# Output stores moved from the SyncE to the GpSimd DMA queue in an FFT-mixing and gated-convolution kernel, with a new instruction order

## The chip, the cores and the metric

The kernel runs on one core of a Trainium2 chip. The core has a matrix engine (TensorE, PE in the profile; its weight loads are PEld), a vector engine (VectorE, DVE), a scalar engine (ScalarE, ACT), GpSimd (POOL) and a synchronisation engine (SyncE, SP), which computes nothing and here only issues DMA transfers. Sixteen DMA engines move the data between the chip's main memory (HBM) and the core's on-chip memory (SBUF); the matrix engine writes to accumulators (PSUM). The metric is the device time of one execution in microseconds (us), as the median of several runs.

## The reference

The input `x` has 8 batches of 3200 positions by 256 channels in float32. Two blocks follow each other. The first is a global filter: a real FFT along the positions, a multiplication with a complex filter, and the inverse FFT. The second is a gated linear unit with a causal convolution of 5 taps per channel:

```python
X = np.fft.rfft(x, axis=1)
y = np.fft.irfft(X * (filt_r + 1j * filt_i)[None], n=3200, axis=1)     # first block

yp = np.concatenate([zeros(B, 4, D), y], axis=1)                       # second block
gate_pre = sum(conv_w[k] * yp[:, k:k + S, :] for k in range(5))
gate = 1 / (1 + np.exp(-gate_pre))
out = (gate * (y @ w_val)) @ w_out                                     # float32
```

## The kernel before, in words

The FFT of 3200 points is done as 100 x 32 by matrix products with tables made on the chip. A batch runs through these stages; the short names are those of the planner and of the rank tables.

Input stages: `lx` loads x in 8 pieces of 100 partitions (`load_x`, L197; the DMA at L200 converts float32 to bfloat16) into one of 10 buffers `xt`. `s1` (PE, L467) is the product of length 100 with the tile's full 128 rows, `so` copies its result out of PSUM (ACT L458 or DVE L460), `t` transposes it on DVE (L486), `s2` (PE, L496, tiles of 64 x 64) is the product of length 32, `xs` copies it out. `z` (DVE, L512) multiplies with the filter.

Inverse stages: `ia` (PE, L527, 64 x 64) undoes the product of length 32, `ue` copies it out into `u`. The data then has to change its partitions. Batch 0 does that with a DVE transpose; batches 1 to 7 write `u` to a scratch tensor in HBM in 7 transfers (`wr`, `escr`, L550) and read it back in 8 pieces of two transfers each (`lv`, `vt`, L560 and L561). `ib` (PE, L578) is the inverse product of length 100, `ye` (ACT, L587) copies it to `yt`, whose halo of 4 columns GpSimd clears (`ha`, L594).

Output stages, in blocks of 512 positions, 7 per batch (the last has 128): `cv` (PE, L627, tiles of 32 x 32; the short block L613) is the convolution with diagonal tables, `ga` (ACT, L637) the sigmoid, `vl` (PE, L647) the product with `w_val`, `gv` (DVE, L662) the gate times it, `op` (PE, L670) the product with `w_out`, `oe` copies it out of PSUM into one of 4 buffers `o` (ACT or DVE), and `store` (L682; the DMA at L685) writes it to HBM, 512 KB for a full block.

The order is planned in Python when the kernel is built. `Plan` (L42) simulates the engines: each task has an engine or a choice of two (ACT or DVE for copies), an estimated duration, dependences, buffers that it takes and gives back, and a rank. Whenever an engine is free, the ready task of lowest rank goes next, and each engine's instructions are written out in that order; each engine then executes them strictly in order and waits where something isn't ready. The ranks are `8*batch + LAG[stage] + STEP[stage]*n`, with `FIRST` added for batch 0. `STAY` is added to a PE task whose tile shape (mode 0, 1 or 2 for full, 64 and 32) differs from the last one's, `LEAN` to a copy put on DVE. `CONV` is the planned duration of a convolution. DMA transfers are modelled too: issuing costs the issuing engine's time, and the transfer then occupies one resource `DQ` for its estimated duration. Its `mode` there tells the issuing queue, 0 for SP and 1 for POOL, and a transfer of the queue that did not go last is preferred. The helper `dma` (L697) adds such a transfer for SP; `dx` (L712) is that of an x load. Real transfers are not bound to this model.

Before the change POOL issues the x loads (and the filters and weights at the start), and SP issues scratch writes, scratch loads and output stores. An issuing engine that waits for a buffer or for a result holds back everything behind it in its order.

Of the kernel before, what the change touches and what calls it, by code (L numbers as in the profile page):

```python
# [20 lines left out]
NV = 4 * NS  # L21
TURN = (0,)

LAG = dict(lx=-196.5, s1=-215.5, so=-54.5, t=9.5, pd=-50, s2=-219, xs=-44.5, z=193.5, ia=60,
           ue=52.5, k=-194, ib=97, ye=-272, cv=79.5, ga=-241.5, vl=-22, gv=-253.5, op=152,
           oe=-151)
FIRST = dict(lx=-125.5, s1=102, so=31.5, t=257, pd=29, s2=41, xs=-256, z=-217, ia=-4.5, ue=25,
             k=20.5, ib=113, ye=135, cv=-14.5, ga=-103.5, vl=78, gv=-43.5, op=126, oe=145)
CONV = 1.14
STEP = dict(lx=0, s1=2.15, so=0.4, t=0.4, pd=0.3, s2=1.9, xs=0.4, z=0.8, ue=0.2, k=2.2, ib=2.45,  # L30
            ye=0.5, cv=2.4, ga=2, vl=1.15, gv=1.9, op=1.35, oe=0)
STAY, LEAN = 30.5, 87.5
RC = 4
NCH = R // RC
UCH = [(m, min(2, NM - m)) for m in range(0, NM, 2)]
# [104 lines left out]
def kernel(  # L140
# [21 lines left out]
    nc = tc.nc  # L162
# [6 lines left out]
    DQ = D // E  # L169
# [22 lines left out]
    st = {}  # L192
# [489 lines left out]
    def store(b, c):  # L682
        o = st.pop(("O", b, c))
        w = width(c)
        nc.sync.dma_start(  # L685
            out=out[b, BLK * c:BLK * c + w, :].rearrange("(p r) d -> p (r d)", p=128),
            in_=o[:, 0:w // 128 * D])

# [3 lines left out]
    add = plan.add  # L692
# [1 line left out]
    def two(a, v):  # L694
        return {"ACT": a, "DVE": v}

    def dma(name, us, rank, dep, give=(), land=2.0):  # L697
        add(name, {"DQ": us}, rank, dep, None, land=land, mode=0)
        add(name + "+", {"none": 0.0}, rank, [name], None, give=give)

    for b in range(B):
        turned = b in TURN
        t0 = NCH * b

        def at(stage, n=0, b=b, t0=t0):
            return t0 + LAG[stage] + (FIRST.get(stage, 0) if b == 0 else 0) + STEP.get(stage, 1) * n

        for j in range(NCH):
            if b:
                add(f"lx{b},{j}", {"POOL": 0.6}, at("lx", j), ["hold"],  # L710
                    lambda e, b=b, j=j: load_x(b, j), take=("xt",), land=1.5)
                add(f"dx{b},{j}", {"DQ": 1.15}, at("lx", j), [f"lx{b},{j}"], None, land=2.0, mode=1)  # L712
            dep = [f"dx{b},{j}"] if b else [f"x0{j}", "cfa"]
            dep = dep + ([f"s1{b},{j - 1}"] if j else [])
            add(f"s1{b},{j}", {"PE": 0.45}, at("s1", j), dep, lambda e, b=b, j=j: s1(b, j),
                ps=1, take=("so",) if j == 0 else (), give=("xt",), mode=0)
            add(f"so{b},{j}", two(0.93, 1.14), at("so", j), [f"s1{b},{j}"],
                lambda e, b=b, j=j: so(b, j, e), free=[(f"s1{b},{j}", 0)])
        for q in range(4):
            add(f"t{b},{q}", {"DVE": 1.17}, at("t"), [f"so{b},{j}" for j in range(NCH)]  # L720
                + ([f"t{b},{q - 1}"] if q else []),
                lambda e, b=b, q=q: turn(b, q), take=("t",) if q == 0 else (),
                give=("so",) if q == 3 else ())
        add(f"pd{b}", {"POOL": 1.2} if turned else {"none": 0.0}, at("pd"),
            ["pool"] + ([f"pd{b - 1}"] if b else []),
            lambda e, b=b: pad(b), take=("u",) if turned else ("u", "e"))
        for u, (m0, nm) in enumerate(UCH):
            half = 0 if m0 + nm <= FCUT[0][1] else 1
            add(f"s2{b},{u}", {"PE": 0.11 * nm}, at("s2", u), ["wa"]
                + [f"t{b},{q}" for q in range(4)] + ([f"s2{b},{u - 1}"] if u else []),  # L730
                lambda e, b=b, u=u: s2(b, u), ps=1, take=("xs", "z"),
                give=("t",) if u == len(UCH) - 1 else (), mode=1)
            add(f"xs{b},{u}", two(0.13 + 0.4 * nm, 0.04 + 0.55 * nm), at("xs", u),
                [f"s2{b},{u}"], lambda e, b=b, u=u: xs(b, u, e), free=[(f"s2{b},{u}", 0)])
            add(f"z{b},{u}", {"DVE": 0.06 + 0.55 * nm}, at("z", u), [f"xs{b},{u}", f"fl{half}"],
                lambda e, b=b, u=u: zed(b, u), give=("xs",))
            add(f"ia{b},{u}", {"PE": 0.22 * nm}, at("ia", u),
                [f"z{b},{u}", f"te{u // 2},1", f"pd{b}"],
                lambda e, b=b, u=u: inva(b, u), ps=1, give=("z",), mode=1)
            add(f"ue{b},{u}", two(0.13 + 0.4 * nm, 0.04 + 0.55 * nm), at("ue", u),  # L740
                [f"ia{b},{u}"], lambda e, b=b, u=u: ue(b, u, e), free=[(f"ia{b},{u}", 0)])
            if not turned:
                add(f"wr{b},{u}", {"SP": 0.45}, at("ue", u), [f"ue{b},{u}"],
                    lambda e, b=b, u=u: wr(b, u), land=1.0)
                dma(f"wq{b},{u}", 0.38 * nm, at("ue", u), [f"wr{b},{u}"])
        if turned:
            for q in range(4):
                add(f"k{b},{q}", {"DVE": 1.87}, at("k"), [f"ue{b},{u}" for u in range(len(UCH))]
                    + ([f"k{b},{q - 1}"] if q else []),
                    lambda e, b=b, q=q: back(b, q), take=("v",) if q == 0 else (),  # L750
                    give=("u",) if q == 3 else ())
        else:
            add(f"wd{b}", {"none": 0.0}, at("ue"), [f"wq{b},{u}+" for u in range(len(UCH))],
                None, take=("v",), give=("u",))
            for j in range(NCH):
                add(f"lv{b},{j}", {"SP": 0.8}, at("ib", j) - 2, [f"wd{b}"],
                    lambda e, b=b, j=j: lv(b, j), land=1.0)
                dma(f"lq{b},{j}", 0.6, at("ib", j), [f"lv{b},{j}"])
        for j in range(NCH):
            add(f"ib{b},{j}", {"PE": 0.37}, at("ib", j),  # L760
                [f"k{b},3" if turned else f"lq{b},{j}+", "cim"]
                + ([f"ib{b},{j - 1}"] if j else []),
                lambda e, b=b, j=j: ib(b, j), ps=1, take=("y",) if j == 0 else (),
                give=(("v",) if turned else ("v", "e")) if j == NCH - 1 else (), mode=0)
            add(f"ye{b},{j}", {"ACT": 0.79}, at("ye", j), [f"ib{b},{j}"],
                lambda e, b=b, j=j: ye(b, j), free=[(f"ib{b},{j}", 0)])
        add(f"ha{b}", {"POOL": 0.2}, at("ib"), [f"ye{b},0"], lambda e, b=b: halo(b))
        for c in range(NB):
            f = width(c) / BLK
            if c == NB - 1:  # L770
                add(f"cv{b},{c}", {"PE": 0.28}, at("cv", c),
                    [f"ye{b},{j}" for j in range(NCH)] + [f"ha{b}", "dg0", "dg1"],
                    lambda e, b=b, c=c: conv(b, c), ps=1, take=("g",), mode=1)
            elif c % 2 == 0:
                add(f"cv{b},{c}", {"PE": CONV}, at("cv", c),
                    [f"ye{b},{j}" for j in range(NCH)] + [f"ha{b}", "dg0", "dg1"],
                    lambda e, b=b, c=c: conv(b, c), ps=2, take=("g", "g"), mode=2)
            p = c // 2 * 2
            add(f"ga{b},{c}", {"ACT": 0.77 * f + 0.16}, at("ga", c), [f"cv{b},{p}"],
                lambda e, b=b, c=c: gate(b, c), free=[(f"cv{b},{p}", c % 2)])  # L780
            add(f"vl{b},{c}", {"PE": 0.87 * f}, at("vl", c),
                [f"cv{b},{p}"] + ([f"vl{b},{c - 1}"] if c else []), lambda e, b=b, c=c: val(b, c),
                ps=1, take=("gv",), give=("y",) if c == NB - 1 else (), mode=0)
            add(f"gv{b},{c}", {"DVE": 1.08 * f + 0.06}, at("gv", c),
                [f"vl{b},{c}", f"ga{b},{c}"], lambda e, b=b, c=c: gv(b, c), give=("g",),
                free=[(f"vl{b},{c}", 0)])
            add(f"op{b},{c}", {"PE": 0.88 * f}, at("op", c), [f"gv{b},{c}"],
                lambda e, b=b, c=c: outp(b, c), ps=1, take=("o",), give=("gv",), mode=0)
            add(f"oe{b},{c}", two(0.77 * f + 0.16, 1.08 * f + 0.06), at("oe", c),
                [f"op{b},{c}"], lambda e, b=b, c=c: oe(b, c, e), free=[(f"op{b},{c}", 0)])  # L790
            add(f"st{b},{c}", {"SP": 0.5}, at("oe", c), [f"oe{b},{c}"],
                lambda e, b=b, c=c: store(b, c), land=1.0)
            dma(f"sq{b},{c}", 1.2 * f, at("oe", c), [f"st{b},{c}"], give=("o",))
    add("pool", {"none": 0.0}, -100, [], None, land=20.0)
    add("wts", {"POOL": 5.0}, 8.5, ["hold"], lambda e: load_w())
    for j in range(NCH):
# [65 lines left out]
```

## Time and profile before

| What | Value |
| --- | --- |
| Median of 3 runs | 313.03 us (312.55, 313.03, 317.41) |
| Profiled execution: its time | 311.8 us |
| its span, from the first to the last instruction | 310.0 us |
| PE, DVE, ACT, POOL busy | 253.6, 265.0, 244.9, 59.4 us |
| mean granted TensorE clock | 0.963 |
| DMA engines' busy share, SP's queue q1 | 50.3% (51.79 MB) |
| DMA engines' busy share, POOL's queue q0 | 31.0% (15.31 MB) |
| Output stores | 48 of 512 KB and 8 of 128 KB, issued by SP from 79.1 to 305.6 us |
| x loads | 64 of 200 KB, issued by POOL from 1.5 to 176.2 us |

Busy times are of one profiled execution. In the profile `DVE z L512` is a group of instructions by engine, the tile that it writes and its line in the kernel; an arrow `<-` in a list of waits reads "waited for"; SPq and POOLq are DMA-issuing instructions of those engines. The first 60 us hold the making of tables, the filters and the first batch's way in; PE is busy for 36.56 us of them. From 300 us on only the last output blocks remain.

### The profile page before, as it was taken

The numbers are of one execution on the slowest core, as the hardware profiler recorded it, in microseconds if no ns is written. First come the engines' busy times: TensorE is split into PE (matmuls) and PEld (weight loads), VectorE is DVE, ScalarE is ACT, GpSimd is POOL, SyncE is SP. The second block draws the span as 40 slices with busy tenths as digits, with TensorE's granted clock in tenths as the row PEclk, the third lists the DMA queues.
The fourth block names the chain that finished last, engine by engine and source line by source line (L and its number), as shares of the span: only waits on it lengthen the run. The fifth ranks groups of instructions, "written<-read, shape, count | busy, mean of one in ns | idle before, by whom it ended". The sixth has DMA issues, their size and how long they took to land.

```text
span 310.0 us, 10810 instructions
## 1 busy us (share of the span) xinstructions
PE 253.6 (82%) x4616; PEld 157.5 (51%) x4644; DVE 265.0 (85%) x294; ACT 244.9 (79%) x291; POOL 59.4 (19%) x123
## 2 busy tenths in 40 slices
PE   2832779788986799998959969999899989899992
PEld 0121516344544535664547336655666556667661
DVE  7789898899896979999979968999999999285672
ACT  3963889997895888899959957997878789869652
POOL 8773658510230032002300400000000000000000
PEclk9999986999997699999999998999999999999998
DMA  6998699999799969957999978963874789785656
GB/s 98 182 188 157 101 174 123 165 194 239 252 220 243 326 147 239 289 205 171 196 276 327 241 145 266 293 224 118 259 242 164 270 261 294 260 286 191 262 221 237
DMA packets 53520, 67.79 MB, mean 219 GB/s; under 512 B 7840, under 2 KB 34336, under 8 KB 53472
## 3 DMA queue, kind: packets, MB, share of 16 engines
q1 hardware_dynamic: 41264, 51.79, 50.3%
q0 software_dynamic: 12208, 15.31, 31.0%
q8 instruction: 36, 0.59, 0.7%
q14 instruction: 12, 0.10, 0.1%
HBM read 42.54 MB, written 38.14 MB: 260 GB/s over the span
## 4 chain that ended last, share of the span: by engine, by line
PE 34%; DMA 23%; DVE 20%; ACT 8%; issue 7%; POOL 4%; SPq 2%; DVEq 0%; ACTq 0%; POOLq 0%
DMA vt<-escr 9%; PE ps L647 8%; PE ps L670 8%; DMA xt<-in_x_dram 7%; PE ps L627 7%; DVE z L512 6%; DVE gv L662 5%; PE ps L578 4%; PE ps L527 3%; DVE tt L486 3%; PE ps L467 3%; POOL xt L200 2%; ACT gt L637 2%; DVE xs L460 2%; DMA f_t<-in_filt_i_dram 2%
## 5 line engine op out<-in xcount | busy, mean ns | idle before, releaser
L662 DVE TENSOR_TENSOR gv<-ps,gt 128x1024 bf16<-128x1024 f32 (+1 forms) x56 | 61.1, 1103 | 13.0 <-PE ps L647 11.2
L637 ACT ACTIVATE gt<-ps 128x1024 bf16<-128x1024 f32 (+1 forms) x56 | 50.0, 935 | 18.2 <-PE ps L627 16.8
L512 DVE TENSOR_TENSOR z<-xs,f_t 128x2048 bf16<-128x2048 bf16 (+1 forms) x56 | 62.6, 1141 | 0.5 <-ACT xs L458 0.2
L587 ACT ACTIVATE yt<-ps 128x800 bf16<-128x800 f32 x64 | 51.8, 851 | 8.2 <-PE ps L578 5.9
L670 PE MATMUL ps<-wo_t,gv 128*128 128x256 bf16 x400 | 52.0, 274 | 6.5 <-issue 5.2
L200 POOL DMA_DIRECT2D xt<-in_x_dram x64 | 35.4, 557 | 100.8 <-PE ps L467 93.1
L467 PE MATMUL ps<-xt,cf_t 100*128 100x512 bf16 x128 | 44.0, 433 | 12.3 <-DMA xt<-in_x_dram 8.0
L647 PE MATMUL ps<-yt,wv_t 128*128 128x512 bf16 (+1 forms) x196 | 51.4, 356 | 2.2 <-ACT gt L637 0.4
L458 ACT ACTIVATE u<-ps 128x1024 bf16<-128x1024 f32 (+1 forms) x39 | 39.0, 1009 | 12.2 <-PE ps L527 7.9
L670 PEld LDWEIGHTS <-gv 128*128 128x128 bf16 x400 | 37.5, 98 | 16.3 <-issue 9.3
L458 ACT ACTIVATE so<-ps 128x1024 bf16<-128x1024 f32 x39 | 38.8, 1040 | 5.7 <-PE ps L467 5.3
L486 DVE STREAM_TRANSPOSE tt<-so 128x1024 f32<-128x1024 f32 x32 | 39.0, 1234 | 2.0 <-ACT so L458 2.0
L578 PE MATMUL ps<-ci_t,vt 104*128 104x100 f16 (+1 forms) x512 | 35.0, 219 | 7.1 <-DMA vt<-escr 5.2
L458 ACT ACTIVATE xs<-ps 128x1024 bf16<-128x1024 f32 (+1 forms) x38 | 35.9, 975 | 5.5 <-PE ps L496 5.0
L527 PE MATMUL ps<-z,a_t 64*64 64x256 bf16 x416 | 30.5, 309 | 9.7 <-DVE z L512 9.0
L627 PE MATMUL ps<-yt,dg_t 32*32 32x512 bf16 x1920 | 35.9, 387 | 3.1 <-issue 1.3
L578 PEld LDWEIGHTS <-vt 104*128 104x128 bf16 (+1 forms) x512 | 29.3, 104 | 16.7 <-DMA vt<-escr 6.5
L458 ACT ACTIVATE o<-ps 128x1024 f32<-128x1024 f32 (+1 forms) x34 | 32.7, 973 | 6.2 <-PE ps L670 5.0
L460 DVE CAST so<-ps 128x1024 bf16<-128x1024 f32 x25 | 30.1, 1226 | 3.5 <-PE ps L467 3.2
L460 DVE COPY o<-ps 128x1024 f32<-128x1024 f32 (+1 forms) x22 | 22.7, 1033 | 12.0 <-PE ps L670 12.0
L627 PEld LDWEIGHTS <-dg_t 32*32 32x32 bf16 x1920 | 24.1, 88 | 14.5 <-issue 11.0
L496 PE MATMUL ps<-tt,w_t 64*64 64x256 bf16 x416 | 22.8, 298 | 8.8 <-DVE tt L486 5.8
(98 smaller groups left out, 209.6 us busy)
## 6 DMA issues: line engine op xcount, KB each, us to landing
out_dram<-o SPq DMA_DIRECT2D x48, 512.0 KB
xt<-in_x_dram POOLq DMA_DIRECT2D x64, 200.0 KB, 7.7
escr<-u SPq DMA_DIRECT2D x42, 256.0 KB
vt<-escr SPq DMA_DIRECT2D x56, 192.0 KB
out_dram<-o SPq DMA_DIRECT2D x8, 128.0 KB
f_t<-f_t SPq DMA_DIRECT2D x4, 224.0 KB
escr<-u SPq DMA_DIRECT2D x7, 128.0 KB
vt<-escr SPq DMA_DIRECT2D x56, 16.0 KB
```

The source lines that it names most:

```text
L458: nc.scalar.activation(dst, src, AF.Copy, **kw)
L460: nc.vector.tensor_copy(dst, src)
L467: nc.tensor.matmul(ps[:, 512 * h:512 * h + 512], lhsT=cf_t[0:L].rearrange("p h c i -> p (h c i)"), rhs=xv[:, DQ // 2 * h:DQ // 2 * h + DQ ...
L486: nc.vector.transpose(dst, src)
L512: nc.vector.tensor_tensor(z[:, :, :, 0:nm * D], st.pop(("XS", b, u))[:, :, 0:nm * D].unsqueeze(1) .to_broadcast((128, 2, 2, nm * D)), f_t[ ...
L578: nc.tensor.matmul(ps[:, o:o + L], lhsT=v[rows, RC * j + a, 128 * dh:128 * dh + 128], rhs=ci_t[rows, way, :], start=True, stop=True)
L587: nc.scalar.activation(y[:, :, H:H + N].rearrange("p h (a r) -> p h a r", r=R)[:, :, :, RC * j:RC * j + RC], ps[:, :].rearrange("p (h n) - ...
L627: nc.tensor.matmul(two[s][o:o + 32, 512 * dh:512 * dh + BLK], lhsT=dg_t[rows, dh, k, 32 * (i % 2):32 * (i % 2) + 32], rhs=y[rows, dh, p:p ...
L637: nc.scalar.activation(g[:, :, 0:w], two_banks(ps, w), AF.Sigmoid)
L647: nc.tensor.matmul(ps[:, 512 * eh:512 * eh + w], lhsT=wv_t[:, dh, eh, o:o + 128], rhs=y[:, dh, H + BLK * c:H + BLK * c + w], start=(dh == ...
L662: nc.vector.tensor_tensor(o, i0, i1, op=ALU.mult)
L670: nc.tensor.matmul(ps[:, D * a:D * a + D], lhsT=gv_[:, eh, 128 * a:128 * a + 128], rhs=wo_t[:, c % 2, eh, :], start=(eh == 0), stop=(eh == 1))
```

## The change

The output stores are issued by GpSimd instead of SyncE, in the code and in the planner's model, where they now belong to the queue of the x loads (mode 1) and cost POOL 0.6 us each. The planner's durations of transfers are changed: a scratch write from 0.38 to 0.44 us per unit, a scratch load from 0.6 to 0.68, an x load from 1.15 to 1.22, a full store from 1.2 to 1.35, and the time from the end of a transfer to its use (`land`) from 2.0 to 2.3 us. The convolution's duration goes from 1.14 to 1.2. All ranks and both penalties have new values. The work of each instruction stays the same.

```diff
-LAG = dict(lx=-196.5, s1=-215.5, so=-54.5, t=9.5, pd=-50, s2=-219, xs=-44.5, z=193.5, ia=60,
-           ue=52.5, k=-194, ib=97, ye=-272, cv=79.5, ga=-241.5, vl=-22, gv=-253.5, op=152,
-           oe=-151)
-FIRST = dict(lx=-125.5, s1=102, so=31.5, t=257, pd=29, s2=41, xs=-256, z=-217, ia=-4.5, ue=25,
-             k=20.5, ib=113, ye=135, cv=-14.5, ga=-103.5, vl=78, gv=-43.5, op=126, oe=145)
-CONV = 1.14
-STEP = dict(lx=0, s1=2.15, so=0.4, t=0.4, pd=0.3, s2=1.9, xs=0.4, z=0.8, ue=0.2, k=2.2, ib=2.45,
-            ye=0.5, cv=2.4, ga=2, vl=1.15, gv=1.9, op=1.35, oe=0)
-STAY, LEAN = 30.5, 87.5
+LAG = dict(lx=-147, s1=-200, so=-45.5, t=83.5, pd=-169, s2=-234, xs=85, z=333, ia=84, ue=99.5,
+           k=-230.5, ib=160, ye=-273, cv=166.5, ga=-280, vl=-12, gv=-150.5, op=173.5, oe=-166.5)
+FIRST = dict(lx=-94, s1=96.5, so=15, t=352.5, pd=14.5, s2=36.5, xs=-310, z=-267, ia=-7.5,
+             ue=-59, k=7.5, ib=123.5, ye=150, cv=12.5, ga=-115.5, vl=58, gv=-74.5, op=87,
+             oe=220.5)
+CONV = 1.2
+STEP = dict(lx=0.7, s1=0.1, so=2.1, t=2.5, pd=1.6, s2=0, xs=2.2, z=1.05, ia=2.5, ue=0.75, k=0.1,
+            ib=2.5, ye=0.1, cv=2.4, ga=0.5, vl=2.05, gv=0, op=2.5, oe=1.8)
+STAY, LEAN = 4, 111
@@ store
-        nc.sync.dma_start(
+        nc.gpsimd.dma_start(
             out=out[b, BLK * c:BLK * c + w, :].rearrange("(p r) d -> p (r d)", p=128),
             in_=o[:, 0:w // 128 * D])
@@ planner: transfers
-    def dma(name, us, rank, dep, give=(), land=2.0):
-        add(name, {"DQ": us}, rank, dep, None, land=land, mode=0)
+    def dma(name, us, rank, dep, give=(), land=2.3, mode=0):
+        add(name, {"DQ": us}, rank, dep, None, land=land, mode=mode)
         add(name + "+", {"none": 0.0}, rank, [name], None, give=give)
...
-                add(f"dx{b},{j}", {"DQ": 1.15}, at("lx", j), [f"lx{b},{j}"], None, land=2.0, mode=1)
+                add(f"dx{b},{j}", {"DQ": 1.22}, at("lx", j), [f"lx{b},{j}"], None, land=2.0, mode=1)
...
-                dma(f"wq{b},{u}", 0.38 * nm, at("ue", u), [f"wr{b},{u}"])
+                dma(f"wq{b},{u}", 0.44 * nm, at("ue", u), [f"wr{b},{u}"])
...
-                dma(f"lq{b},{j}", 0.6, at("ib", j), [f"lv{b},{j}"])
+                dma(f"lq{b},{j}", 0.68, at("ib", j), [f"lv{b},{j}"])
...
-            add(f"st{b},{c}", {"SP": 0.5}, at("oe", c), [f"oe{b},{c}"],
+            add(f"st{b},{c}", {"POOL": 0.6}, at("oe", c), [f"oe{b},{c}"],
                 lambda e, b=b, c=c: store(b, c), land=1.0)
-            dma(f"sq{b},{c}", 1.2 * f, at("oe", c), [f"st{b},{c}"], give=("o",))
+            dma(f"sq{b},{c}", 1.35 * f, at("oe", c), [f"st{b},{c}"], give=("o",), mode=1)
```

## The prediction

> **What bounds the kernel now.** I read the page first (busy shares, slices, DMA queues), then busy time by stage, the wait lists, the timeline around the longest stalls, and last the DMA by queue and packet. The page's first and third part:
>
> ```profile
> PE 253.6 (82%) x4616; PEld 157.5 (51%) x4644; DVE 265.0 (85%) x294; ACT 244.9 (79%) x291; POOL 59.4 (19%) x123
> ...
> q1 hardware_dynamic: 41264, 51.79, 50.3%
> q0 software_dynamic: 12208, 15.31, 31.0%
> ```
>
> Three compute engines and the DMA engines stand near 80% each; only POOL is idle. By stage:
>
> ```profile
> 60.00:300.00 240.00, 212.94 (x4163) 136.55 (x4190) 210.09 (x197) 198.02 (x230) 19.56 (x41) 0.97 0.81 236
> ...
> 220.00:240.00 20.00, 18.74 (x367) 13.08 (x365) 20.00 (x20) 16.29 (x21) 0.10 (x1) 1.00 0.63 215
> 260.00:280.00 20.00, 18.78 (x414) 13.34 (x416) 11.34 (x12) 15.79 (x19) 0.10 (x1) 1.00 0.82 278
> ```
>
> The columns are the window and its length, then PE, PEld, DVE, ACT and POOL busy, the clock, the DMA share and GB/s. From 60 to 300 us PE is busy 212.94 of 240 us, so 27 us are idle; DVE is full in the middle and loses its load from 260 on, where PE runs at 18.78 of 20. No single engine is the bound: the order decides how well the loads overlap. How much of those 27 us is the DMA's? The wait lists say little:
>
> ```profile
> PE ps L578 <- DMA vt<-escr: 5.2, 5, 3.1
> ...
> ACT u L458 <- DMA vt<-escr: 3.8, 1, 3.8
> ```
>
> That is total, times and longest (60 to 300 us): PE waits 5.2 us for scratch loads, 3.1 of it once. The chain's 9% for `vt<-escr` is mostly covered by other work. The one long wait, in the timeline:
>
> ```profile
> 84.02 0.37 SPq L685 DMA_DIRECT2D out_dram<-o  x1
> ...
> 95.58 0.55 PE L578 MATMUL ps<-ci_t,vt 104*128 104x100 f16 x8 [3.09 <-DMA vt<-escr]
> ```
>
> A store was put into SP's queue at 84.02 among batch 1's scratch loads while x loads were running. PE, DVE and ACT then all have a gap of about 3 us at 92 to 96.
>
> **The change, part by part.** Durations are those of the profiled execution: span 310.0, its time 311.8 us (1.8 around the span). The runs shown have a median of 313.03, so 1.2 is added at the end.
>
> (1) *Stores leave SP's DMA queue.* Queues share the engines packet by packet:
>
> ```profile
> q0 software_dynamic: 550, 0.85, 64.5%
> q1 hardware_dynamic: 510, 0.85, 37.8%
> ```
>
> This is 113 to 121 us, x loads on q0 and scratch loads on q1, both in 2 KB pieces: equal bytes, one packet each in turn (414 and 415 by the packet records; the surplus is 4-byte semaphore writes). A store is 128 packets of 4 KB, 8 per engine, with a median of 161 ns, so 1.3 us alone. Ahead of a scratch load in q1, with an x packet (173 ns) between every two, it costs 8 x (161+173) ns = 2.7 us; moved to q0 it takes turns with the scratch instead. So the 3.09 us gap loses 2.7. Other loads queued behind stores run without x loads (185 us on), landing 3 to 4 us after issue, and PE waits hardly at all. **-2.7 us**, bounds 0 and -9.0 (all of 5.2+3.8).
>
> The Trainium skill, DMA: Bandwidth & Descriptors, Issuing engines are not separate DMA queues, speaks against this: DMAs of all issuers run on the same 16 engines, so several issuers save sequencer time alone. By it this term is 0. The trace agrees on the shared engines (64.5%+37.8% fill them), but shows turns between queues, which the section's rule does not price.
>
> (2) *SP's issue time.* 56 stores x 354 ns = 19.8 us leave SP, and its waits for `o` (29.1 us for ACT, 28.7 for DVE):
>
> ```profile
> SPq L685 <- ACT o L458: 29.1, 21, 2.8
> SPq L685 <- DVE o L460: 28.7, 13, 4.8
> ...
> SPq L561 <- DMA out_dram<-o: 4.6, 3, 2.3
> ```
>
> What stood behind them are scratch writes and loads, whose lateness term 1 already counts. SP computes nothing: 0. If that cover fails, the gain is within term 1's -9.0.
>
> (3) *POOL's issue time.* 56 more issues of 0.552 us (its median for x loads) = 30.9 us on an engine with 250 us idle: 0. Each store is now a wait in POOL's order. Behind it stand x loads and the 0.12 us halo memset that the convolution needs. x loads have slack: they are issued as the previous batch's buffers come free, some 20 us before use, and of PE's 8.0 us waiting for them 5.5 fall before the first matmul. If a store's 4.8 us wait at SP reappeared before the halo, it would cost up to that once per batch, but the memset is issued after the first of eight `ye` copies, and the other seven are 0.85 us each: 6 us of cover.
>
> (4) *Later landing.* The first packet of an SP store follows its issue by 0.83 us, that of a lone x load by 1.25 to 1.46; the issue itself is 0.55 instead of 0.35. At the end nothing covers it: the last `o` copy ends near 305 us and the span 5 us later. **+0.6 us** (0.4 to 1.2).
>
> (5) *Stores behind x loads on q0.* Eight of the 56 stores fall where x loads are in flight:
>
> ```profile
> DMA to landing us min/median/max: 3.5/7.7/12.4
> ```
>
> That is an x load's landing; an SP store's last packet comes 2.99 us (median) after issue. There are four `o` buffers, each held until its store lands. In this kernel the store of 84.02 took 8.8 us and no engine waited for `o`, so I take **0**; bound: 8 x (7.7-3.0) us / 4 buffers = +9.4. POOL also uses eight completion semaphores in turn; in the startup its DMAs wait for the one eight earlier (0.25 to 0.62 us each), and with stores among x loads that comes sooner. It is inside that bound.
>
> (6) *The new order.* All ranks change, but the sequence of priorities hardly does: on PE s2, s1, vl, ia first, then cv, ib, op before and ib, cv, op after; DVE still takes gv and the output copy first and z last. Two things do change. op comes within 14 of ib (before 55), so outputs need not pile up at the end. And the penalty for changing PE's tile mode falls from 30.5 to 4. The nearest rows: between two groups of matmuls of one mode the next starts 0.16 to 0.26 us before the last's modelled end, between modes 0.07 before: 0.1 to 0.2 us per change. The trace has 152 changes among 379 transitions; if all changed it would be 227 x 0.14 = +32. Against this stand the 27 us that PE idles between 60 and 300. With one end at -27 and the other at +32, and readiness rather than rank deciding most steps in both, I take **0**, and +-10 for the range (a third of either end).
>
> Sum: 311.8 - 2.7 + 0.6 = 309.7; with the 1.2 to the median 310.9, **311**.
>
> **Rivals.** *Nothing moves*: the gap of 3 us stays because the engines are full around it whichever queue holds the store, term 1 is 0, and 311.8+0.6+1.2 = 313.6. For it: the DMA engines are 81% busy from 60 to 300. Against it: the one-for-one turns. It is the case that the Trainium skill's section named above describes.
>
> *The order fits better*: DVE idles 8.7 us in 260 to 280 while PE is full, and PE idles in the middle. If a third of the 27 us is recovered because longer transfer times let outputs be placed earlier, another 9 go, less the 1 to 2 already counted: 303. For it: every engine has 45 us or more of idle time in the span. Against: DVE is already at 20.0 of 20 in places.
>
> *Output buffers*: term 5's bound comes true, 311+9.4 = 320. Place: the `oe` copies on ACT and DVE, in order, so that everything behind stops. It decides from the point where a fifth output copy comes within the landing time of four stores: in the end phase 15 stores are issued in 27 us, 7.2 us per four, against about 5 of copy, issue and landing; beside x loads 8 to 9 would exceed it.
>
> *Mode changes*: 70 more switches of 0.14 us on a full PE, 311+10 = 321. Against: the planner still charges 0.1 per change.
>
> **How the numbers follow.** Forecast 311: 0.34. Nothing moves: 0.13. Better order, 303: 0.27. Output buffers, 320: 0.15. Mode changes, 321: 0.11. Two per cent of 313 is 6.3 us, about what separates a difference from none here: below 306.8 is faster, 0.27; 306.8 to 319.3 the same, 0.47; above, slower, 0.26. The forecast's own range is 307 to 316. The 8-in-10 range reaches into both sides: 302 to 322.
>
> **What would show it.** Right: the gap near 92 gone, `PE <- vt` under 3 us, SP waiting only for `u` and scratch, no wait for an `o` buffer, store landings of 3 to 4 us outside x bursts, the last store ending about 0.6 later. Wrong: ACT or DVE waiting on stores (term 5), POOL holding x loads until PE waits for them (term 3), more mode changes, or PE's idle time from 60 to 300 us far from 24 (term 6, the step I trust least).

## The result and the profile after

The changed kernel takes **315.21 us** (median of 20 runs, 312.63 to 319.88), the kernel before 313.03 (20 runs, 309.72 to 317.41). The ratio is **1.0082, 95% interval 1.0053 to 1.0111**: 0.8% slower, where 0.7% faster was forecast. Here and below a time is the median of all runs, while a ratio compares only runs within 1.5% of each kernel's fastest, since some executions are slower, and so it can differ from the quotient of two medians. The profiled execution has a span of 315.1 us and took 316.83, so it lies 1.6 above its median, while that of the kernel before lay 1.2 below its own. Of the 5.1 us between the two spans nearly 3 are thus a matter of these two executions.

Busy times and DMA queues of the changed kernel, from its page:

```profile
PE 255.1 (81%) x4644; PEld 155.2 (49%) x4644; DVE 259.8 (82%) x289; ACT 249.9 (79%) x296; POOL 89.6 (28%) x179
...
q0 software_dynamic: 19504, 41.53, 52.1%
q1 hardware_dynamic: 33200, 25.57, 27.2%
```

The stores' 26 MB have gone from q1 to q0, POOL carries 30 us more, and 5 us of copies have gone from DVE to ACT. By stage (window and length, then PE, PEld, DVE, ACT, POOL busy, clock, DMA share, GB/s):

```profile
60.00:300.00 240.00, 212.28 (x4159) 134.14 (x4153) 204.38 (x192) 201.05 (x232) 46.88 (x93) 0.98 0.79 233
220.00:240.00 20.00, 18.40 (x347) 12.18 (x340) 19.96 (x18) 18.25 (x22) 1.69 (x4) 1.00 0.67 224
260.00:280.00 20.00, 17.52 (x404) 11.62 (x394) 12.15 (x13) 14.55 (x18) 3.16 (x7) 1.00 0.82 279
```

From 60 to 300 us PE is idle for 27.7 us, against 27.1 before: nothing was gained there in sum. Yet the wait that the change was to remove has gone. In the changed kernel's list of waits from 60 to 300 us PE doesn't wait for scratch loads at all. Apart from 0.2 us of PEld, the only wait for them that is left in the list (total, times, longest) is this:

```profile
ACT u L458 <- DMA vt<-escr: 2.4, 2, 2.0
```

The longest of POOL's waits, in the same form:

```profile
POOL out_dram L685 <- ACT o L458: 118.5, 27, 15.3
```

POOL now stands waiting for output blocks, which costs nothing: neither ACT nor DVE waits for an `o` buffer, and PE waits 0.2 us in all for x loads after 60 us. In their place stand gaps of PE without a releaser, one of them in the timeline of PE:

```profile
186.74 0.42 PE L627 MATMUL ps<-yt,dg_t 32*32 32x512 bf16 x11 [2.93 <-issue]
```

### The profile page after: what moved, and what is told of

Same layout as the page of the kernel before. It is cut to its first block, busy times and chain, and to the rows that moved or that the text cites. A ratio compares the mean times of both kernels' runs of the same rounds, so it can differ in the third digit from the quotient of the medians.

```text
span 315.1 us, 10866 instructions
## 1 busy us (share of the span) xinstructions
PE 255.1 (81%) x4644; PEld 155.2 (49%) x4644; DVE 259.8 (82%) x289; ACT 249.9 (79%) x296; POOL 89.6 (28%) x179
## 4 chain that ended last, share of the span: by engine, by line
PE 29%; DVE 21%; issue 16%; DMA 16%; ACT 8%; POOL 6%; SPq 2%; POOLq 0%; DVEq 0%; ACTq 0%
PE ps L647 8%; DMA xt<-in_x_dram 7%; PE ps L627 6%; DVE z L512 6%; PE ps L670 5%; PE ps L527 4%; DVE gv L662 3%; DVE so L460 3%; ACT gt L637 3%; DVE o L460 3%; DVE tt L486 2%; DVE xs L460 2%; DMA vt<-escr 2%; DMA f_t<-in_filt_r_dram 2%; POOL out_dram L685 2%
## 5 line engine op out<-in xcount | busy, mean ns | idle before, releaser
L685 POOL DMA_DIRECT2D out_dram<-o x56 | 30.1, 538 | 166.7 <-ACT o L458 118.5
L637 ACT ACTIVATE gt<-ps 128x1024 bf16<-128x1024 f32 (+1 forms) x56 | 49.1, 934 | 13.5 <-PE ps L627 11.4
L647 PE MATMUL ps<-yt,wv_t 128*128 128x512 bf16 (+1 forms) x224 | 53.8, 364 | 4.0 <-issue 1.4
L467 PE MATMUL ps<-xt,cf_t 100*128 100x512 bf16 x128 | 44.9, 444 | 10.6 <-DMA xt<-in_x_dram 7.8
L458 ACT ACTIVATE u<-ps 128x1024 bf16<-128x1024 f32 (+1 forms) x39 | 38.0, 976 | 15.7 <-PE ps L527 13.1
L458 ACT ACTIVATE so<-ps 128x1024 bf16<-128x1024 f32 x45 | 44.6, 1026 | 6.3 <-PE ps L467 5.6
L670 PEld LDWEIGHTS <-gv 128*128 128x128 bf16 x400 | 38.0, 98 | 12.3 <-issue 2.9
L458 ACT ACTIVATE o<-ps 128x1024 f32<-128x1024 f32 (+1 forms) x34 | 33.5, 992 | 9.7 <-PE ps L670 9.1
L527 PE MATMUL ps<-z,a_t 64*64 64x256 bf16 x416 | 28.8, 295 | 14.5 <-DVE z L512 11.9
L458 ACT ACTIVATE xs<-ps 128x1024 bf16<-128x1024 f32 (+1 forms) x37 | 34.6, 969 | 4.8 <-PE ps L496 3.8
L578 PE MATMUL ps<-ci_t,vt 104*128 104x100 f16 (+1 forms) x512 | 33.5, 214 | 2.0 <-ACT u L458 1.0
L647 PEld LDWEIGHTS <-wv_t 128*128 128x128 bf16 x224 | 19.6, 98 | 23.2 <-issue 9.1
```

The costliest lines, as they stand in the source:

```text
L458: nc.scalar.activation(dst, src, AF.Copy, **kw)
L467: nc.tensor.matmul(ps[:, 512 * h:512 * h + 512], lhsT=cf_t[0:L].rearrange("p h c i -> p (h c i)"), rhs=xv[:, DQ // 2 * h:DQ // 2 * h + DQ ...
L527: nc.tensor.matmul(ps[64 * h:64 * h + 64, 512 * t + D * a:512 * t + D * a + D], lhsT=tab[rows, h, m0 + a, :], rhs=z[rows, w, h, D * a:D * ...
L578: nc.tensor.matmul(ps[:, o:o + L], lhsT=v[rows, RC * j + a, 128 * dh:128 * dh + 128], rhs=ci_t[rows, way, :], start=True, stop=True)
L637: nc.scalar.activation(g[:, :, 0:w], two_banks(ps, w), AF.Sigmoid)
L647: nc.tensor.matmul(ps[:, 512 * eh:512 * eh + w], lhsT=wv_t[:, dh, eh, o:o + 128], rhs=y[:, dh, H + BLK * c:H + BLK * c + w], start=(dh == ...
```

## The experiments

**Order and queue apart.** Two orders (old and new) and two issuers of the stores (SyncE and GpSimd) give four kernels; the kernel before and the changed kernel are two of them. The third is the old order with the stores on GpSimd, the planner untouched (in `store` of the kernel before):

```diff
-        nc.sync.dma_start(
+        nc.gpsimd.dma_start(
```

> Only the issuing engine of the store changes (GpSimd instead of SyncE); every engine's order is that of the kernel before, also on PE, ACT and DVE. Theory A (the moved queue gains, the new order loses): the PE gap of 3.1 us near 92 us falls below 1 us, PE waits under 3 us for scratch loads after 60 us, and the ratio to the kernel before is 0.990 to 0.995 (310 to 311.5 us). Theory B (stores on GpSimd cost more than they give: later landing, stores and x loads in one order): ratio 1.005 or more, with ACT or DVE waiting for o buffers or PE for x loads. Theory C (the queue is worth nothing either way, since the DMA engines are shared): ratio 0.998 to 1.003 and the gap near 92 us stays at 2.5 us or more.

Measured: 313.62 us against 311.96, ratio 1.0073 (1.0034 to 1.0111). The gap near 92 us is gone, as theory A had it. The timeline of PE in this kernel at the place where the kernel before stood still for 3.09 us:

```profile
92.92 0.51 PE L578 MATMUL ps<-ci_t,vt 104*128 104x100 f16 x8
93.27 1.26 PE L670 MATMUL ps<-wo_t,gv 128*128 128x256 bf16 x10
94.36 0.52 PE L578 MATMUL ps<-ci_t,vt 104*128 104x100 f16 x8
```

But the kernel is slower all the same, so A's figure is wrong. B's ratio came out, but none of B's signs is there (no wait for `o`, none of PE for x after 60 us). As all orders but SP's and POOL's are equal, the two traces can be laid on each other instruction by instruction. The lead of this kernel over the kernel before grows by 3.1 us at 98 us, is lost by 1.7 at 268 (a gap of PE of 2.37 us instead of 0.70) and by another 1.7 in the tail.

The fourth kernel is the new order with SyncE's stores (in `store` of the changed kernel):

```diff
-        nc.gpsimd.dma_start(
+        nc.sync.dma_start(
```

> The changed kernel with its stores issued by SyncE again, in the planned order: the new order alone. Theory A: slower than the changed kernel by what the queue gains, ratio to the kernel before 1.012 to 1.018 (317 to 319 us), with waits of PE for scratch loads that the changed kernel doesn't have. Theory B: faster than the changed kernel, ratio 0.995 to 1.003. Theory C: the same as the changed kernel, ratio 1.005 to 1.011.

Measured: 318.05 us, ratio 1.0238 (1.0185 to 1.0292), theory A and somewhat beyond. PE's waits for scratch loads are there, in this kernel's list from 60 to 300 us:

```profile
PE ps L578 <- DMA vt<-escr: 6.3, 3, 4.2
```

In the new order the queue is worth 1.5%; with SyncE's stores PE waits 6.3 us for scratch loads there, with GpSimd's not at all. Without the queue, the new order would have lost 2.4%.

**Other orders.** The changed kernel with the ranks and penalties of the kernel before (LAG, FIRST, STEP, CONV, STAY, LEAN), planner durations and queue as changed:

> Stores on GpSimd and the planner's new durations, but the ranks and penalties of the kernel before: a third order, planned with the measured durations. If it is the new ranks that lose (theory A in its narrow form), the ratio to the kernel before is 0.990 to 0.998. If longer planned transfers are what loses, it is 1.005 to 1.010 like the changed kernel. If orders scatter by a per cent or more whatever they are planned with, it lies anywhere from 0.985 to 1.02, with other places for the PE gaps of over 1 us.

Measured: 315.2 us, ratio 1.0117 (1.0062 to 1.0171). The new ranks are not what loses. The changed kernel with one penalty back:

```diff
-STAY, LEAN = 4, 111
+STAY, LEAN = 4, 87.5
```

> The changed kernel with the penalty for copies on DVE back at 87.5 (from 111): a neighbouring order of the new ranks. If the moved load (DVE busy 5 us less, ACT 5 us more than before) is what loses, the ratio to the kernel before falls to 0.998 to 1.003 and ACT is busy under 248 us. If it isn't, 1.005 to 1.011. If orders scatter, a change as small as this one moves the time by more than 0.5 per cent without a change in busy times that explains it.

Measured: 1.011 (1.0041 to 1.0178), with the same gaps of PE at the same places. But ACT is busy 249.5 us with 296 instructions, against 249.9 with 296 in the changed kernel: the edit did not move the load back, so this kernel doesn't tell whether the shifted load loses. The kernel with the old order and GpSimd's stores tells a part of it: it has the old load (ACT 244.8, DVE 265.4 us) and loses 0.7% all the same.

**The tail.** From the end of the last copy into `o` to the end of the span it was 4.9 us before and 6.0 after. The last stores of the kernel before, in SP's timeline (start, length, merged):

```profile
300.51 5.46 SPq L685 DMA_DIRECT2D out_dram<-o  x5
```

Those of the changed kernel, in POOL's timeline:

```profile
309.46 1.07 POOL L685 DMA_DIRECT2D out_dram<-o  x2 [1.03 <-ACT o L458]
```

The last copies end at 305.11 and 309.17. SP issues the last store 0.45 us later, at 305.56; POOL issues two in a row, the second 0.82 later, at 309.99. The last packet lands 2.5 to 2.6 us after issue in both, and the span ends 1.9 us after it before, 2.6 after. So two terms of about 0.4 and 0.7 us. To test it, the last batch's stores went back to SyncE, first in the old order (in `store`):

```diff
-        nc.sync.dma_start(
+        (nc.gpsimd if b < 7 else nc.sync).dma_start(
```

> The order of the kernel before; stores of batches 0 to 6 on GpSimd, those of the last batch on SyncE. The tail from the last copy of an output block to the end of the span was 4.9 and 5.1 us with stores on SyncE and 6.0 to 6.6 us in four kernels with stores on GpSimd. Theory D (the tail is what the move costs in the old order): the tail falls to 5.0 us and the ratio from 1.007 to 1.002 or 1.003. Theory E (the cost lies in the middle, in POOL's order or in instruction fetches of PE that fall elsewhere): the tail falls to 5.0 us, but the ratio stays at 1.005 or more.

Measured: 310.38 us, equal to the kernel before in the same series, ratio 0.9978 (0.9939 to 1.0016), 0.95% below all stores on GpSimd; the tail is 4.7 us instead of 6.6. Theory D holds, with more than the tail's own 1.9 us. Then in the new order:

> The changed kernel with the stores of the last batch on SyncE. The tail from the last output copy to the end falls from 6.0 to 5.0 us. If the tail is a cost of its own, the ratio to the kernel before falls from 1.008 to 1.004 or 1.005; if the order's middle hides or takes it, it stays at 1.007 or more.

Measured: ratio 1.0039 (1.0000 to 1.0078), 0.4% below the changed kernel, tail 4.3 us. The tail is a cost of its own in both orders, 0.8 to 1.9 us by the traces of one and the same order.

**The one store.** Only batch 0's seven stores on GpSimd, with every instruction of PE, DVE and ACT in the old order:

```diff
-        nc.sync.dma_start(
+        (nc.gpsimd if b == 0 else nc.sync).dma_start(
```

> The order of the kernel before; only the seven stores of batch 0 on GpSimd, among them the one at 84 us that stands ahead of scratch loads beside x loads. Theory D: the PE gap of 3.1 us near 92 us falls below 1 us, the tail stays at 5.0 us, and the ratio is 0.990 to 0.996. Theory E: ratio 0.998 to 1.004, the gap's gain is taken back by other gaps. If the gap of the one profiled execution of the kernel before is not typical of it, the gain is also under 0.3 per cent.

Measured: 307.99 us against 310.38, ratio 0.9956 (0.9918 to 0.9993); the gap near 92 is gone, the tail 4.4 us. The same kernel once more:

> The old order with only batch 0's seven stores on GpSimd, timed again: ratio 0.992 to 0.999, the PE gap near 92 us gone, tail 4.4 to 5.0 us. If the first measurement was luck, 0.999 to 1.003.

Measured: 307.59 us against 312.27, ratio 0.9893 (0.9828 to 0.9957), below the range that was expected. Batches 0 to 2:

> The old order with the stores of batches 0 to 2 on GpSimd. If only the store near 84 us matters, the ratio is that of batch 0 alone, 0.989 to 0.996. If each further store on GpSimd costs something, it lies between that and the 0.998 of batches 0 to 6.

Measured: 309.34 us against 311.94, ratio 0.9922 (0.9879 to 0.9965). All three measurements beat the kernel before, by 1.4 to 3.3 us. About 0.5 us of that is a shorter tail (4.4 us instead of 4.9, with SyncE issuing the last stores in both); why is not shown. Nor was the store of 84 us moved alone: three more of batch 0 were issued at 79 us. In its list of waits from 60 to 300 us the repeat has no wait of PE for scratch loads; PEld keeps one:

```profile
PEld L578 <- DMA vt<-escr: 0.4, 2, 0.2
```

**How far one execution stands for the others.** The kernel before, profiled twice more:

> The kernel before, unchanged, profiled once more: how far the filters' arrival (hold at 33.1 us in the first profile, 34.1 to 35.5 in five others), the gap of 3.1 us near 92 us, and PE's gaps at instruction fetches (2.6 us at 156 and at 182) move from one execution to the next. If the start is a matter of the kernel, hold is at 33 us again; if of the execution, anywhere from 33 to 35.5. The gap near 92 is expected within 0.5 us of 3.1.

> The kernel before, unchanged, profiled a third time, for the same three readings: hold at 33 or up to 35.5 us, the gap near 92 us within 0.5 us of 3.1, and the fetch gaps of PE at 156 and 182 us at 2.6 us or moved.

Measured: `hold`, which waits for the filters, at 35.0 and 33.5 us (33.1 in the first profile), so the start moves by 2 us from one execution to the next in one and the same kernel, and the 1.8 us by which the changed kernel's profile started later say nothing. The gap near 92 us was 2.5 us, just outside what was expected, and 3.1 us; the gaps without a releaser came to 1.9 and 2.5 us (at 156 and 182) and 2.9, 2.0 and 1.5 (at 156, 184, 271).

**Gaps of PE without a releaser.** The instruction queue q8 of the page brings 36 packets of 16 KB. In the packet records the gaps of 1.2 us and more that the page calls "issue" end 1.1 to 1.7 us after such a packet has arrived: in the kernel before, packets end at 157.57 and 183.31 and PE goes on at 158.90 and 184.86. To see whether they belong to a position in PE's stream or to a place in the order, small products whose results are overwritten were put ahead of batch 0's first s2, where PE waits for the filters anyway:

```diff
+        if b == 0 and u == 0:
+            for _ in range(32 // 4):
+                for h, t in ((0, 0), (1, 1), (0, 1), (1, 0)):
+                    rows = slice(64 * h, 64 * h + 64)
+                    nc.tensor.matmul(ps[64 * t:64 * t + 64, 512 * h:512 * h + 16],
+                                     lhsT=w_t[rows, NM * t, :], rhs=t_[rows, 0:4, NM * t, :],
+                                     start=True, stop=True)
```

> The changed kernel with 32 small matrix products repeated ahead of the first s2 of batch 0, whose results the real ones overwrite: 64 more PE instructions (a weight load and a product each) in a stretch where PE waits for the filters. Every later PE instruction keeps its order and stands 64 places further in the stream. Theory F (PE's gaps of 1 us and more without a releaser are waits for the next 16 KB of its instructions, 256 of them): they end 1.1 to 1.7 us after a packet of the instruction queue as before, but lie elsewhere, 64 instructions earlier in the order, the sum over the span moves from 9.5 us to something between 3 and 12, and the span moves with it. Theory G (the gaps belong to places of the order, behind convolutions): they stay behind the same instructions near 71, 157, 184, 247 and 273 us, and the time stays at a ratio of 1.008.

The same with 64 and with 96 products:

> As the kernel with 64 more PE instructions, with 128 (64 small products). Theory F: the gaps lie half a 16 KB block away from those of the changed kernel, none of its five gaps stays at its instruction, and the time follows their sum. Theory G: gaps and time stay as in the changed kernel, ratio 1.008, or 1.01 if the products themselves cost 0.5 us.

> As the kernel with 64 more PE instructions, with 192 (96 small products). Theory F: another set of gaps, and among the three shifts the shortest time goes with the smallest sum of these gaps; their spread in time is 1 to 2 per cent. Theory G: all three alike within 0.4 per cent.

Measured, with PE's matrix products counted from the start: in the changed kernel the gaps stand ahead of products 607, 2007, 2387, 3531 and 4039; in the old order with GpSimd's stores ahead of 2007, 2387 and 4039; in the kernel with 64 more instructions ahead of 607, 2007, 2387 and 4039 again (and of 1498), although the work there stands 32 products further. The timeline of PE in that kernel at product 2387:

```profile
180.64 1.10 PE L634 MATMUL ps<-yt,dg_t 32*32 32x512 bf16 x42
184.82 1.49 PE L634 MATMUL ps<-yt,dg_t 32*32 32x512 bf16 x43 [3.09 <-issue]
```

And in the old order with GpSimd's stores, at the same product:

```profile
180.78 0.49 PE L670 MATMUL ps<-wo_t,gv 128*128 128x256 bf16 x3
182.16 0.71 PE L670 MATMUL ps<-wo_t,gv 128*128 128x256 bf16 x5 [0.89 <-issue]
```

(Line 634 is the convolution, 627 in the other kernels.) The gaps stay at their positions in the stream, a multiple of 128 products (256 instructions) apart but for a few other instructions of PE, and not at their work. So they are waits for the next block of instructions, as theory F says, and with 64 more instructions each lies 64 instructions earlier in the order. What F said of the time came out in part. The three kernels have one and the same order, and their medians are 315.75, 312.49 and 314.39 us with 64, 128 and 192 more instructions, against 312.67 for the kernel before: a spread of 1%, as F says, not under 0.4% as G does. But the shortest time does not go with the smallest sum. The sums of these waits after 50 us are 10.3 us in the changed kernel, 10.5, 8.2 and 7.2 in the three. (The ratios, 0.9977 (0.9928 to 1.0026), 0.9953 (0.9891 to 1.0015) and 1.0082 (1.0044 to 1.0120), rest on 5, 4 and 11 of 12 runs. The twelve runs with 64 more spread evenly from 310.2 to 319.7 us, so its ratio decides nothing.) With 128 instructions more, the changed order is thus as fast as the kernel before: a part of what it loses seems to be a matter of where its instructions lie in the stream, and not of which goes first.

**Is any new plan slower?** Three plans with SyncE's stores, each from one edit to the planner of the kernel before:

```diff
-CONV = 1.14
+CONV = 1.2
```

> The kernel before with one planner constant changed: the planned convolution takes 1.2 instead of 1.14 us. Stores on SyncE, ranks as before; the order is a new one on every engine. Theory S (the old order is a good one out of a scatter of about a per cent, and a new plan loses on average): ratio 1.004 to 1.02. Theory M (the planned durations of transfers are what loses, the scatter is small): ratio 0.997 to 1.003.

```diff
-STAY, LEAN = 30.5, 87.5
+STAY, LEAN = 28, 87.5
```

> The kernel before with the penalty for changing PE's tile mode at 28 instead of 30.5, nothing else: again a new order on every engine. Theory S: ratio 1.004 to 1.02, by another amount than with the other constant. Theory M: 0.997 to 1.003.

The third has the five planned durations of transfers from the changed kernel and nothing else of it:

> The kernel before with the measured durations of the transfers in its planner (0.44, 0.68, 1.22, 1.35 and 2.3 us), stores on SyncE, ranks as before. Theory S: ratio 1.004 to 1.02 like the two kernels with one constant changed. Theory M: slower than those two by 0.5 per cent or more. If the measured durations help as they were meant to, below 1.

Measured: 1.0118 (1.0061 to 1.0175), 1.0061 (1.0018 to 1.0105) and 0.9965 (0.9923 to 1.0008). So the three plans scatter by 1.5%, and two that differ by a constant that means next to nothing lose 1.2 and 0.6%, as theory S has it. The third does not: the measured durations do not lose, and whether they gain is not clear of the noise. Of the plans tried the old order is among the better. The measured durations even took away most of the gap near 92 us without moving a queue; the list of waits of that kernel from 60 to 300 us:

```profile
PE ps L578 <- DMA vt<-escr: 2.7, 4, 1.1
```

Last, that order with batch 0's stores on GpSimd:

> The order planned with the measured durations (SyncE's stores in the plan), but batch 0's seven stores issued by GpSimd. If the two gains are one (both only take the store out of the way of batch 1's scratch loads near 92 us, and that order's wait there is 1 us already), the ratio is 0.993 to 0.998, as without the move. If they add up, 0.985 to 0.992, with PE's waits for scratch loads falling from 2.7 us to under 1.

Measured: 309.96 us against 311.94, ratio 0.9950 (0.9917 to 0.9982). PE's waits for scratch loads are gone, but the time is that of the plan alone, as expected if the two gains are one.

| Order | Stores on GpSimd | Ratio to the kernel before | 95% interval |
| --- | --- | --- | --- |
| old | none | 1 | |
| old | all | 1.0073 | 1.0034 to 1.0111 |
| old | batches 0 to 6 | 0.9978 | 0.9939 to 1.0016 |
| old | batches 0 to 2 | 0.9922 | 0.9879 to 0.9965 |
| old | batch 0 | 0.9956; 0.9893 | 0.9918 to 0.9993; 0.9828 to 0.9957 |
| new | all (the change) | 1.0082 | 1.0053 to 1.0111 |
| new | batches 0 to 6 | 1.0039 | 1.0000 to 1.0078 |
| new | none | 1.0238 | 1.0185 to 1.0292 |
| old ranks, measured durations | none | 0.9965 | 0.9923 to 1.0008 |
| old ranks, measured durations | batch 0 | 0.9950 | 0.9917 to 0.9982 |

## Why the prediction was wrong

The sum was 311.8 - 2.7 + 0.6 + 0 + 1.2 = 310.9, put as 311; the result is 315.2. Against the kernel before the terms make -2.1 us, and the ratio of 1.0082 is +2.6 us. The experiments take the change apart. Each step is the difference of two ratios, times 312 us; the ratios are known to within 0.3 to 0.7%, 1 to 2 us, so that the small steps are not clear of noise.

| Step | Forecast, us | Measured, us |
| --- | --- | --- |
| batch 0's stores to GpSimd, old order (term 1) | -2.7 | -1.4 and -3.3 (batches 0 to 2: -2.4) |
| those of batches 1 to 6 too, old order (terms 2, 3, 5) | 0 | +0.7 or +2.7, by which of the two is taken |
| the last batch's too (term 4) | +0.6 | +3.0 in the old order, +1.3 in the new |
| the new order (term 6) | 0 | +0.3 with all stores on GpSimd, +1.9 with batches 0 to 6, +7.4 with none |

Two steps failed: term 4 was too small, and term 6 was put at nothing. How much falls to each depends on which half of the change is taken first, since moving all stores gains 1.5% in the new order and loses 0.7% in the old.

*Term 1 was right.* The 3.09 us gap came from stores ahead of scratch loads in one queue. It goes in every kernel that takes batch 0's stores out of the queue. The rival "nothing moves" falls with it. In the new order, moving all stores was worth 4.9 us (1.5%), within the term's bound. That the size fits in the old order is in part luck: one packet each in turn holds for 113 to 121 us as a whole, but from 114 to 119 us it was 266 x packets to 245 of scratch, and from 116 to 120 us 166 to 291, so the turns are not strict. The Trainium skill (DMA: Bandwidth & Descriptors, Issuing engines are not separate DMA queues) says that issuing from several engines saves only issue time. For the sum of the transfers the traces agree, with 236 GB/s before and 233 after from 60 to 300 us; for a transfer that others wait for they don't, since the gap went.

*Terms 2, 3 and 5* show none of the waits that they name: in the changed kernel and in the old order with all stores on GpSimd, no engine waits for SP's or POOL's order, ACT and DVE not for `o`, and PE not for the halo. The rival of the output buffers falls, though a store beside x loads took up to 12.3 us from issue to landing (median 4.0). Waits for `o` of 1.5 us came up with batch 0 alone on GpSimd and of 1.6 us with the old ranks in the changed planner. Whether the terms were right at 0 in time is not shown: the stores of batches 1 to 6 seem to cost something, and no wait tells what.

*Term 4 was mis-sized.* Forecast +0.6 with a bound of 1.2; the tail shows +1.0 (changed kernel) to +1.7 (old order), and timed, the last batch's stores are worth 0.4% in the new order and 0.95% in the old, 1.3 and 3.0 us. What failed is that only the last store's own issue and first packet were counted. A lone store's first packet did come 1.10 us after its issue instead of 0.83. But the store also waits behind another store's issue of 0.53 us, and the end of the program after the last packet takes 2.6 us instead of 1.4 to 2.1.

*Term 6 failed in its reason.* The prediction has "readiness rather than rank deciding most steps" and so lets the order cost nothing. With SyncE's stores, where the order is held against the old one without the queue, the new order loses 2.4%, and one constant moved by 5 or 8% lost 1.2 and 0.6%. That is inside the +-10 us given to the term, but its middle was wrong: of the five orders timed with SyncE's stores the old one is the second best, and the other four lie at a mean of 1% above it. A new plan should have been put at half a per cent to one per cent of loss until something speaks for it. Of the two prices named for it, mode changes are refuted: 160 instead of 152, 8 x 0.14 = 1 us. The rival "the order fits better" is refuted as well.

*What stays open.* The traces say where PE stands in the new order: waits for instruction blocks of 9.4 to 10.3 us after 50 us in three kernels with the new order and stores on GpSimd, 4.8 to 7.8 in eight executions of the old order. But PE's idle time from 60 to 300 us is nearly the same, 27.7 and 27.1 us, and kernels with 1 to 3 us of instruction waits were both above the kernel before (1.0117, 1.0061) and below it (0.9965). So this is no sufficient cause.

For the old order with all stores on GpSimd, -3.1 in the gap, +1.7 in the tail and +1.7 at 268 us make +0.3 us where 2.3 were measured, and the kernel with the last batch on SyncE is 3 us (0.95%) faster than it with a tail shorter by 1.9. About 2 us of its 2.3 are not accounted for by a named wait. The granted clock may be a part of that: it averaged 0.956 over this kernel's ten runs and 0.963 over the fifteen of the kernel before beside them, and among 119 runs of the kernel before those with 0.01 less clock took 1.4 us longer (correlation -0.63), which would make 1 us by this estimate. For the changed kernel the clock explains little: 0.960 over its 20 runs, 0.959 to 0.964 in five series of the kernel before.

## What to carry to other kernels

A store ahead of a latency-critical load in one queue costs the reader the store's packets and whatever takes turns with them, here a gap of 3.1 us: move the stores of that place, not all, and leave the last ones on the issuer whose end is shorter. The seven stores of batch 0 alone gave -0.4 and -1.1%; with all 56 it was +0.7%. And judge a change of queue with the order held still: the four new plans timed with SyncE's stores moved the time by -0.4 to +2.4%.

## What the runs showed of the hardware

PE runs out of instructions. Its 9288 loads and products come in 16 KB blocks of 256 instructions. Where a block ends in a convolution, or within 50 products behind one, PE can stand for up to 3.9 us and goes on 1.1 to 1.7 us after the block's packet has landed. A convolution's 160 instructions (80 products) are through in 1.3 us. How fast the block ahead was used up tells where: in the nine kernels whose traces hold every product, 288 block ends can be placed from the gaps' spacing, and all 31 waits of 0.9 us or more stand behind 128 products that took under 5 us (64 ends are such, 15 of the 18 under 3 us have the wait). The Trainium skill (Runtime: NRT & Kernel Launch, Instruction fetch mechanics) has the 16 KiB blocks and calls the cost of crossing into the next mostly hidden; here it isn't, behind bursts of 32 x 32 tiles. The positions are fixed in the stream, so a changed order meets other work there.

Two queues share the DMA engines in small turns: 414 x packets and 415 scratch packets in the same 8 us. And from the last packet to the program's end 2.6 us pass in the seven profiles where GpSimd issued the last stores, 1.4 to 2.1 in the other thirteen.
